# Row 0 of an attention and feed-forward kernel in two interleaved halves, with loads in queue order and a chain of released loads

One core of a Trainium2 chip. The metric is the device time of the whole kernel in microseconds (us), lower is better.

## What is computed

Attention over 8 rows of a batch (8 heads, 576 positions, head dimension 64), then a feed-forward product over all 4608 tokens. Cut to what matters:

```python
mask_plain = (rel >= 0) & (rel < 32)                        # heads 0 to 3: "sliding"
mask_dil = (rel >= 0) & (rel < 128) & (rel % 4 == 0)        # heads 4 to 7: "dilated"
attn = softmax(where(mask, q @ k.T / 8, -1e9));  x = attn @ v   # x: 4608 x 512
h = x @ w_in                                                # 512 -> 2048, "mm1"
r = maximum(h, 0); out = (r * r) @ w_out                    # 2048 -> 512, "mm2"
```

The feed-forward part goes by chunks of 512 tokens. Row 0 gives the tokens of chunk 0; attention of a later row runs on TensorE between the feed-forward matmuls of the chunk before it.

## The kernel before

The parts that the change touches (cuts marked with `...`). `idle()` issues filler matmuls whose result nobody uses, `pump(n)` issues the next n pieces of feed-forward work. In the profiles QKTp and QKTd are the transposed q and k of the sliding and the dilated heads, AT the attention weights, an AV product the weights times V, and xT the transposed result that mm1 reads. Half clock is also called cold.

```python
    load_sliding_qk(0, (nc.sync, nc.scalar))
    ...
    load_dilated_qk(0)
    load_sliding_v(0)
    load_dilated_v(0, nc.scalar)
    ...
    cast_sliding_qk(0, (nc.scalar, nc.scalar, nc.vector, nc.gpsimd))
    idle_matmuls(pj, 14, TOKC)
    ...
    transposes_and_scores(0, idle_and_load)     # w_in is issued in here
    scores_dilated(0, idle)
    cast_dilated_v(nc.scalar, DIL)
    xs = [av_sliding(0, 0)]
    ...
    x_dilated(0, 0, ys, False)
    load_sliding_qk(1)
    load_dilated_qk(1)
    g0 = hidden(0)
    pending.append(mm1_part_gen(0, g0, 0, 288))   # mm1 of the first 288 tokens
    zs = []
    for a in range(2):
        pump(1)
        zs.append(av_dilated(0, 1, a))            # ... beside the end of row 0
    ...
    load_w_out()
    pump(1000)
    pending.append(mm1_part_gen(0, g0, 288, TOKC))
    pump(2)
    reload_v(1)                                   # V of row 1
    ...
    cast_sliding_qk(1, (nc.scalar, nc.vector, nc.scalar, nc.vector))
    transposes_and_scores(1, lambda: pump(1))
    ...
    dk = keep_qk(2)                               # q and k of row 2
```

The softmax here doesn't subtract the row's maximum and nothing guards it: scores larger than these inputs give would overflow.

## Time and profile before

| | before |
|---|---|
| time, median of the 3 runs known then | 307.44 us (307.07 to 307.70) |
| the profiled run itself | 308.89 us, span 307.1 us |
| TensorE busy | 96% of the span |
| first mm1 matmul (chunk 0) | 24.84 us |
| first mm1 matmul of chunk 1 | 64.77 us |
| from there to the end of the span | 242.3 us |

From chunk 1 on TensorE sets the pace and the program is nearly the same in both kernels, so a change before chunk 1 can be read from one moment. I call it "the moment".

### The profile page before, as it was taken

The numbers are of one execution on the slowest core, as the hardware profiler recorded it, in microseconds if no ns is written. First come the engines' busy times: TensorE is split into PE (matmuls) and PEld (weight loads), VectorE is DVE, ScalarE is ACT, GpSimd is POOL, SyncE is SP. The second block draws the span as 40 slices with busy tenths as digits, with TensorE's granted clock in tenths as the row PEclk, the third lists the DMA queues.
The fourth block names the chain that finished last, engine by engine and source line by source line (L and its number), as shares of the span: only waits on it lengthen the run. The fifth ranks groups of instructions, "written<-read, shape, count | busy, mean of one in ns | idle before, by whom it ended". The sixth has DMA issues, their size and how long they took to land.

```text
span 307.1 us, 7069 instructions
## 1 busy us (share of the span) xinstructions
PE 295.0 (96%) x2920; PEld 199.0 (65%) x2920; DVE 213.7 (70%) x428; ACT 184.6 (60%) x317; POOL 41.9 (14%) x86
## 2 busy tenths in 40 slices
PE   6789999999899999999999999999999999999995
PEld 2777774444597459745974597459745974684484
DVE  5487682479976697769776977697769775834744
ACT  2586893668933894389438953895389526505610
POOL 4312302006002300230023002300100010000000
PEclk9599999999999999999999999999999999999998
DMA  7999899899979989999859993979520012003004
GB/s 183 249 210 226 142 179 211 186 224 224 276 147 240 266 143 221 226 225 155 178 168 226 152 231 113 228 173 181 142 96 2 0 40 99 2 0 140 0 0 139
DMA packets 83312, 47.91 MB, mean 156 GB/s; under 512 B 67792, under 2 KB 79568, under 8 KB 82896
## 3 DMA queue, kind: packets, MB, share of 16 engines
q1 hardware_dynamic: 75060, 26.12, 41.3%
q0 software_dynamic: 6848, 19.80, 28.3%
q10 hardware_dynamic: 1372, 1.54, 1.8%
q8 instruction: 23, 0.38, 0.5%
q14 instruction: 9, 0.07, 0.1%
HBM read 39.85 MB, written 16.52 MB: 184 GB/s over the span
## 4 chain that ended last, share of the span: by engine, by line
PE 86%; DMA 6%; ACT 3%; SPq 2%; DVE 1%; issue 1%; DVEq 0%; ACTq 0%
PE ph L324 37%; PE pob L374 9%; PE poa L374 9%; PE poe L374 5%; PE poc L374 5%; PE pod L374 5%; DMA sv<-in_v_dram 3%; PE paw L621 3%; PE ph L302 3%; DMA sq<-in_k_dram 2%; SPq L106 2%; PE pav L607 2%; PE py L654 2%; PE ps L556 1%; PE px L636 1%; PE po L345 1%
## 5 line engine op out<-in xcount | busy, mean ns | idle before, releaser
L324 PE MATMUL ph<-xT,wi 128*128 128x512 f16 x512 | 115.8, 379 | 0.0
L290 ACT ACTIVATE rt<-ph 128x512 f16<-128x512 f32 x128 | 75.5, 602 | 32.9 <-PE ph L324 32.6
L324 PEld LDWEIGHTS <-wi 128*128 128x128 f16 x512 | 48.2, 98 | 55.1
L294 DVE TENSOR_TENSOR g<-rt 128x1024 f16<-128x1024 f16 x56 | 38.7, 691 | 35.2 <-ACT rt L290 34.9
L374 PEld LDWEIGHTS <-sm 128*128 128x128 f16 x512 | 47.0, 98 | 4.9
L374 PEld LDWEIGHTS <-g 128*128 128x128 f16 x384 | 35.8, 98 | 6.5 <-DVE g L292 1.1
L374 PE MATMUL pob<-T,sm 128*128 128x256 f16 x256 | 32.5, 272 | 0.0
L374 PE MATMUL poa<-wo,g 128*128 128x256 f16 x256 | 32.1, 273 | 0.0
L660 ACT COPY xT<-py 128x576 f16<-128x576 f16 x16 | 10.2, 638 | 25.8 <-PE py L654 25.7
L394 POOL DMA_DIRECT2D out_dram<-otl x6 | 4.5, 756 | 152.2 <-DVE otl L429 152.2
L590 DVE TENSOR_TENSOR x_d<-paw,rcp_d 72x512 f16<-72x512 f32 x32 | 22.0, 686 | 1.1
L528 ACT ACTIVATE AT<-pz 128x576 f16<-128x576 f32 x32 | 19.0, 653 | 2.3 <-PE pz L575 1.8
L528 ACT ACTIVATE AT<-ps 128x576 f16<-128x576 f32 x32 | 19.2, 659 | 0.7 <-PE ps L538 0.3
L642 ACT COPY xT<-px 128x576 f16<-128x576 f16 x16 | 10.2, 640 | 14.7 <-PE px L636 14.7
L529 DVE TENSOR_TENSOR AT<-AT,maskp 128x576 f16<-128x576 f16 x32 | 14.9, 474 | 4.5 <-ACT AT L528 3.6
L302 PE MATMUL ph<-xT,wi 128*128 128x288 f16 (+1 forms) x128 | 16.6, 272 | 0.9 <-ACT xT L660 0.5
L590 DVE TENSOR_TENSOR x_p<-pav,rcp_p 96x512 f16<-96x512 f32 x24 | 16.5, 687 | 0.8
L529 DVE TENSOR_TENSOR AT<-AT,maskd 128x576 f16<-128x576 f16 x32 | 14.1, 456 | 3.4 <-ACT AT L528 2.3
L374 PE MATMUL pod<-T,g 128*128 128x256 f16 x128 | 16.2, 272 | 0.0
L374 PE MATMUL poc<-T,sm 128*128 128x256 f16 x128 | 16.2, 272 | 0.0
L374 PE MATMUL poe<-wo,sm 128*128 128x256 f16 x128 | 16.1, 273 | 0.0
L145 ACT CAST vd<-sd 128x1024 f16<-128x1024 f32 x16 | 16.1, 1070 | 0.0
(99 smaller groups left out, 369.7 us busy)
## 6 DMA issues: line engine op xcount, KB each, us to landing
sv<-in_v_dram SPq DMA_DIRECT2D x40, 128.0 KB, 4.6
sd<-in_v_dram SPq DMA_DIRECT2D x7, 512.0 KB, 5.9
dk<-in_k_dram POOLq DMA_DIRECT2D x12, 288.0 KB, 6.6
dk<-in_q_dram POOLq DMA_DIRECT2D x12, 288.0 KB, 8.2
out_dram<-otl POOLq DMA_DIRECT2D x6, 512.0 KB, 3.6
out_dram<-otu POOLq DMA_DIRECT2D x6, 512.0 KB, 3.7
wi<-in_moe_w_in_dram POOLq DMA_DIRECT2D x2, 1024.0 KB, 12.1
wo<-in_moe_w_out_dram POOLq DMA_DIRECT2D x4, 512.0 KB, 10.1
```

The source lines that it names most:

```text
L145: nc.scalar.copy(o, i)
L290: nc.scalar.activation(rt[:, o, :], ph[:], ACTF.Relu)
L294: nc.vector.tensor_mul(g[:, ffc - 1 : ffc + 1, :], rt, rt)
L302: nc.tensor.matmul(ph[:, 0 : t1 - t0], wi[:, dmk, ffc * P : ffc * P + P], xs[:, dmk, :], start=(dmk == 0), stop=(dmk == NDM - 1),)
L324: nc.tensor.matmul(ph, wi[:, dmk, ffc * P : ffc * P + P], xs[:, dmk, :], start=(dmk == 0), stop=(dmk == NDM - 1),)
L374: nc.tensor.matmul(acc, lhs[:, k, t * P : (t + 1) * P], rhs[:, k, :], start=(first and k == 0), stop=(k == NK - 1), skip_group_check=True,)
L528: nc.scalar.activation(AT[:, u, 0:UW], ps[:, :, 0 : UW // 2], ACTF.Exp, scale=scale)
L529: nc.vector.tensor_mul(AT[:, u, 0:UW], AT[:, u, 0:UW], mask)
L590: nc.vector.tensor_tensor(out=x[0:w], in0=pv[:, :, :, 0:D], in1=rcp[0:w].unsqueeze(3).to_broadcast([w, 2, HH, D]), op=ALU.mult,)
L621: nc.tensor.matmul(pav[:, e, h * (D + 2) : h * (D + 2) + D + 1], AT[:, 4 + h, off : off + P], vd[:, t, 2 * a + e, h, 0 : D + 1], start=Tru ...
L642: nc.scalar.copy(xT[:, 0:2, t0 : t0 + 288], px[:, 0:UW].rearrange("x (c t) -> x c t", c=2),)
L660: nc.scalar.copy(xT[:, 2:4, t0 : t0 + 288].rearrange("x c (i r) -> x c i r", r=DIL), py[:, 0:UW].rearrange("x (c r i) -> x c i r", c=2, r= ...
```

## The change

Its intent: start row 0 as soon as half of its q and k is there, let the second half load meanwhile, and let GpSimd issue each later load when it sees that an earlier one has landed. Core of the diff:

```diff
-    load_sliding_qk(0, (nc.sync, nc.scalar))
+    load_sliding_qk_half(0, 0, nc.sync)
+    load_sliding_qk_half(1, 0, nc.scalar)
...
-    load_dilated_qk(0)
+    load_dilated_qk_half(0)
+    load_dilated_v(0, nc.sync, (0,))
+    load_sliding_v(0, 0, 3)
+    load_sliding_qk_half(1, 1, nc.sync)
+    load_sliding_qk_half(0, 1, nc.sync)
+    load_sliding_v(0, 3, 6)
+    load_dilated_v(0, nc.sync, (1,))
     make_identity(nc, ident)
-    load_sliding_v(0)
-    load_dilated_v(0, nc.scalar)
+    load_dilated_qk_half(1)
...
+    def landed(x):
+        nc.gpsimd.tensor_copy(hold[0 : x.shape[0]], x)
+    (first half: casts, transposes, scores, AV products, with fillers)
+    x_sliding(0, 0, xs, False)
+    idle(6)
+    cast_sliding_qk_half(1, 1, nc.scalar)
+    cast_sliding_qk_half(0, 1, nc.scalar)
+    (second half the same way, with fillers)
+    load_w_out(0, 1)
+    landed(wi[:, NDM - 1, 1023:1024])
+    nc.gpsimd.memset(sq[:, :, :, 0:1], 0.0)
+    load_sliding_qk(1)
+    load_dilated_qk(1)
+    load_w_out(1, 4)
+    landed(wo[:, 3, DM - 1 :])
+    ... memsets of sv and sd
+    load_v(1)
+    landed(wo[:, NFF - 1, DM - 1 :])
+    landed(sd[:, 1, HH - 1, DIL * D - 1 :])
+    dk = keep_qk(2)
     g0 = hidden(0)
-    pending.append(mm1_part_gen(0, g0, 0, 288))
-    ... its pieces between the AV products of row 0
+    pending.append(mm1_gen(0, g0))                # unsplit, after row 0
+    pump(22)
     cast_sliding_qk(1, (nc.scalar, nc.vector, nc.scalar, nc.vector))
...  scores and dilated transposes of row 1 now lie beside mm2
```

Besides, w_in is loaded in four pieces instead of two, V of row 0 is cast on GpSimd alone, and in row 2 two pieces of feed-forward work are issued earlier.

## The prediction

> **What bounds the kernel now.** I read the page first: over the whole span TensorE is busy in 96%, and in the 40 slices only the first two are not full. The second slice (7.7 to 15.4 us) is also the only one with a halved TensorE clock.
>
> ```profile
> PE   6789999999899999999999999999999999999995
> ...
> PEclk9599999999999999999999999999999999999998
> DMA  7999899899979989999859993979520012003004
> ```
>
> From slice 9 on the rows of attention are hidden beside the feed-forward product and TensorE sets the pace: the seven-eighths products and the mm1 of a chunk repeat every 30.9 us in the chain. The change touches that part only by moving two fills in row 2. So what counts is one moment: when the first mm1 matmul of chunk 1 starts. All before it (row 0, chunk 0, row 1) is rewritten, all after it is kept. The timeline, and next to it the first matmuls of chunk 0:
>
> ```profile
> 24.84 0.41 PE L302 MATMUL ph<-xT,wi 128*128 128x288 f16 x2
> ...
> 28.96 7.47 PE L302 MATMUL ph<-xT,wi 128*128 128x288 f16 x64
> ...
> 64.77 7.52 PE L324 MATMUL ph<-xT,wi 128*128 128x512 f16 x34
> ```
>
> The moment is 64.77 us. The chain of waits says what led to the first useful matmuls, and later through row 0:
>
> ```profile
> 0.75 7.51 DMA sq<-in_k_dram
> 8.26 0.03 issue
> 8.28 0.96 DVE early L147
> 9.24 0.05 issue
> 9.29 0.66 PE pt L499 x6
> ...
> 16.66 1.10 ACT AT L528 x2
> ...
> 18.48 2.19 ACT AT L528 x4
> ```
>
> The reader sees 8.3 us of waiting for q and k of row 0, then a cast, then the transposes. The table of windows shows what that wait does to TensorE, and that the DMA engines are full from 3 us on:
>
> ```profile
> 5.00:10.00 5.00, 2.06 (x15) 1.16 (x14) 1.32 (x7) 1.56 (x2) 0.82 (x1) 0.86 1.16 239
> 10.00:15.00 5.00, 5.00 (x61) 4.66 (x60) 1.91 (x4) 2.36 (x4) 2.14 (x4) 0.50 1.19 258
> 15.00:20.00 5.00, 4.45 (x99) 3.85 (x97) 4.13 (x10) 4.13 (x11) 1.27 (x3) 0.96 1.16 211
> ```
>
> Between 10 and 15 us TensorE is busy throughout at clock 0.50: it is its own bound there, for some 3 us more than the same instructions would need at full clock. A third stretch: V of row 1 lands at 54.4 us (18 us after issue), but queued mm2 matmuls fill most of that wait.
>
> **What the Trainium skill says.** "TensorE: Matmul & The Clock Gate", section "What's actually happening", says that the array falls to half clock after an idle window of about 3.4 us and gets it back after a busy one. The trace agrees in kind: the filler matmuls end at 6.35 us, the next starts at 9.29, and the clock is 0.50 from 9 to 15 us; it was lost at about 8.6, so after 2.3 us of idling. "DMA: Bandwidth & Descriptors", section "Issuing engines are not separate DMA queues", says that all issuers share 16 engines. It agrees: with three queues issuing, the total stays at 213 to 295 GB/s from 3 to 20 us; order, not the number of queues, decides what lands first. "GPSIMD Engine Reference", section "4.1 Engine selection", has one-input work on GpSimd at roughly line rate; here GpSimd casts 96x768 in 0.82 us against 0.95 on VectorE, so the V casts moved there cost nothing extra.
>
> **The change part by part.** (1) First loads halved. q and k of half a row are 0.59 MB instead of 1.18. By the rates of the windows (12, 152, 295, 275 GB/s), 1.5 MB had moved at 8.3 us, of which 1.18 were q and k; half of it, 0.74 MB, had moved at 5.0. So q and k land near 5.2 us. VectorE is then held by its setup: it ended at 5.4, and the memset of QKTd grows from 64 to 640 words a partition, some 0.55 us by the rate of the 256-word one (0.27 us): 6.0. The 13 fillers end at 6.1. The first half starts 3.2 us earlier, and the idle gap of 2.9 us is gone, so TensorE stays at full clock: another 3 us of the cold stretch.
>
> (2) Against that, the row now runs as two chains one after the other. I followed the changed order with durations of the trace: cast 0.83 (ScalarE) and 0.95 (VectorE), QKTp copy 0.64 and 0.76, a pair of QKTd copies 0.70 and 0.81, exp 0.60, mask 0.50, normalise 0.90 (0.55 for one tile), xT copy 0.64, 0.4 to 0.5 from a matmul's start to its reader. First half: casts done 6.95, copies 8.1 and 8.4, QKTd 9.75, four exps until 11.45, last mask 12.0. V of it (0.64 MB behind q) should land near 10 and be cast on GpSimd by 11.4 and 12.6. AV products 11.6 to 13.3, xT copy of the sliding part done 15.05. Second half: ScalarE's two casts come after that copy in its order, 15.05 to 16.65; QKTp copies to 17.7 and 18.35; exp 18.35 to 18.95; xT copy 19.6; exp 20.2; mask 20.75; QKTd copies 21.55; two exps to 23.2; mask 23.75; four normalises to 26.9; transposes and xT copy: first mm1 at T0 = 28.0. The other bound is TensorE's own queue: 84 fillers of 128 columns at 0.09 us (five take 0.45) are 7.6 us, about 196 small matmuls some 8 us (six transposes 0.33, eight AV products 0.3, sixteen score products 0.31): from 6.1, T0 = 22. Fillers look chosen near the real waits, so I lean a little below my chain: T0 = 26.7.
>
> (3) Chunk 0 is no longer split. Before, 64 matmuls of 288 columns (52 in 6.17 us, 0.119 each) and 64 of 224 (0.10) are 14.0 us; 64 of 512 (34 in 7.36 us, 0.2165) are 13.9. The split cost nothing in TensorE's time, but it allowed 20 matmuls, 2.4 us, to run before row 0 was finished. This overlap is given up.
>
> (4) The rest up to chunk 1. From the end of the first split part, 36.43, to 64.77 are 28.3 us: 44 short mm1 matmuls (4.4 us), row 1 and mm2. The changed kernel needs the 23.9 without those, plus 13.9 for mm1: chunk 1 starts at T0 + 37.8. Equality with 64.77 is T0 = 27.0. Here the change should also win a little: between 40 and 45 us ScalarE was busy for 5.00 of 5 us with relu, exp and copies together; scores and dilated transposes now lie beside mm2, where it has slack, and the one V wait (VectorE's 5.9 us, under a us of it on TensorE) goes if V of row 1 is released by the first w_out piece near 32 us. I put this at 0.6 us. Sum: 26.7 + 37.8 - 0.6 = 63.9, that is 0.9 us earlier: 307.4 - 0.9 = 306.5.
>
> (5) Released loads: none should be late. w_in is issued near 13 us, and its second half is needed at T0 + 7; the q and k of row 1 are released by the second w_in piece near 22 and need some 11 us at half the rate, against a use at T0 + 9.5; row 2's transposes follow as before.
>
> **The rivals.** First, the author's intent holds in full: T0 near 22 to 24, the two halves really overlap, chunk 1 starts 3 to 5 us earlier, 302.5 to 304.5. For it: the fillers, and 6 us of start and clock that are really there to be had. Against it: each half passes all of exp, mask, AV and normalise, and the ScalarE order puts the second half's casts behind the first half's xT copy. Second, the serial chain holds or gets worse: TensorE waits about 2 us near 20 us between the fillers and the second QKTd copies; as 2.3 us of idling lost the clock before, it can be lost again, which adds 1 to 2 us: T0 28 to 30, 308.5 to 310.5. Third, loads become the bound: sliding V comes in small packets and w_in competes with the last V of row 0. In the kernel before, GpSimd's V casts waited for V until 17.05 us; if V of the second half lands after 23, or the chained releases leave DMA engines idle, each us is paid. The full DMA row speaks for little slack, the 0.72 between 30 and 35 us for some.
>
> **Range and chances.** A low of 302.5 is T0 at 23 with the 0.6 and some more of the later stalls removed; a high of 310.5 is T0 at 29.5 with a further us of waits. Faster by over 2% means under 301.3, chunk 1 at 58.6, T0 under 21.5: below even TensorE's own queue, 0.09. Slower by over 2% means over 313.6, 6 us lost, only by a lost clock and late loads together: 0.05. Within 2%: 0.86.
>
> **What would show it.** Right: first transposes near 6.1 us at full clock; no slice at 0.5; exp of the first half done near 11.5; second casts behind the first xT copy near 15; first mm1 at 26 to 28; first mm1 of chunk 1 at 63 to 65; the rest as long as before (242.3 us). Wrong: the first mm1 under 24 (halves overlap more than I think), a clock of 0.5 near 20 us, a DMA wait ahead of mm1, or a part after chunk 1 that changes by over a us.

## The result

| | before | after |
|---|---|---|
| time, median (range) of 4 runs each | 307.57 us (307.07 to 308.44) | 310.10 us (309.85 to 310.78) |
| profiled run, its span | 308.89 us, 307.1 us | 310.78 us, 309.0 us |
| first mm1 matmul | 24.84 us | 29.27 us |
| the moment | 64.77 us | 66.52 us |
| from the moment to the end | 242.3 us | 242.5 us |

The ratio is 1.0083, with a 95% interval of 1.0054 to 1.0111. A ratio here is the mean time of one kernel's fast runs over that of the other's of the same rounds, so not quite the ratio of the medians quoted. The changed kernel is 0.8% slower, the same by the measure of 2%.

The page of the changed kernel, in 40 slices:

```profile
PE   7759999999989999999999999999999999999995
...
PEclk9796999999999999999999999999999999999999
DMA  8999998799989969899949992999430003003003
```

Its start is earlier, but now there are two cold places (the 7 and the 6 in the row of the clock) instead of one. The DMA row looks as full as before; the windows below show a gap in it. TensorE's timeline (start, duration, engine, line, operation; in brackets the wait before it and what ended it):

```profile
6.42 0.68 PE L566 MATMUL ph<-ident,early 96*128 96x96 f16 x12 [0.54 <-ACT early L166]
7.66 0.42 PE L584 MATMUL pg<-ident,early 72*128 72x72 f16 x8 [0.33 <-DMA early<-in_k_dram]
...
10.32 0.42 PE L584 MATMUL pg<-ident,early 72*128 72x72 f16 x8 [2.01 <-DMA early<-in_q_dram]
...
17.67 0.30 PE L566 MATMUL ph<-ident,early 96*128 96x96 f16 x3 [1.12 <-ACT early L166]
...
22.48 0.97 PE L664 MATMUL pz<-QKTd 64*128 64x72 f16 x16 [1.44 <-DVE QKTd L168]
...
29.27 10.53 PE L359 MATMUL ph<-xT,wi 128*128 128x512 f16 x48
...
45.61 1.47 PE L380 MATMUL po<-wo,g 128*128 128x512 f16 x6
```

The first transposes start at 6.42 us against 9.29 before: the 2.9 us are won. But the first mm1 comes at 29.27 us against 24.84. Between them stand a new wait of 2.0 us for the dilated q, and the waits at 17.67 and 22.48 us for the second half, which began late. ScalarE's timeline shows why:

```profile
12.06 1.19 ACT L599 ACTIVATE AT<-pz 128x576 f16<-128x576 f32 x2 [0.39 <-PE pz L664]
16.25 0.64 ACT L735 COPY xT<-px 128x576 f16<-128x576 f16 x1 [3.00 <-PE px L729]
16.78 1.56 ACT L166 CAST early<-sq 96x768 f16<-96x768 f32 x2
...
23.24 1.19 ACT L599 ACTIVATE AT<-pz 128x576 f16<-128x576 f32 x2 [1.68 <-PE pz L664]
27.96 0.64 ACT L735 COPY xT<-px 128x576 f16<-128x576 f16 x1 [3.53 <-PE px L729]
```

The two casts of the second half stand behind the copy of the first half's result, for which ScalarE waits 3.0 us with nothing to do. The table of windows, cut at the moments where the clock changed (the columns are the window, its length, busy times of PE, PEld, DVE, ACT and POOL, the granted clock, the DMA share, GB/s; the share is packet time over the time of 16 engines and can pass 1):

```profile
8.08:11.49 3.41, 1.40 (x29) 1.03 (x29) 1.16 (x3) 1.72 (x4) 0.00 (x0) 1.00 1.21 214
11.49:14.90 3.41, 3.35 (x49) 3.14 (x47) 3.25 (x6) 1.38 (x3) 2.03 (x2) 0.50 1.24 207
14.90:18.32 3.42, 1.95 (x38) 1.55 (x36) 2.35 (x7) 2.07 (x3) 2.81 (x5) 1.00 0.73 162
18.32:21.73 3.41, 2.42 (x51) 1.91 (x51) 1.42 (x4) 2.85 (x6) 2.90 (x4) 1.00 1.24 205
21.73:25.14 3.41, 2.54 (x39) 2.32 (x40) 2.15 (x7) 1.19 (x2) 0.80 (x3) 0.50 1.24 207
25.14:28.55 3.41, 3.41 (x44) 3.41 (x42) 2.73 (x7) 0.59 (x1) 3.21 (x6) 0.50 1.22 222
```

The clock is at half for 10.2 us up to the moment, against 6.8 us in the kernel before. The DMA share falls to 0.73 from 14.90 to 18.32 us. GpSimd holds w_in until it sees the second half's q (15.46 us) and then takes 3.0 us to issue four pieces from 15.70 us; the kernel before issued w_in at 12.90 us, and its share stayed at 1.12 or more from 13 to 20 us.

### The profile page after: what moved, and what is told of

Same layout as the page of the kernel before. It is cut to its first block, busy times and chain, and to the rows that moved or that the text cites. A ratio compares the mean times of both kernels' runs of the same rounds, so it can differ in the third digit from the quotient of the medians.

```text
span 309.0 us, 6928 instructions
## 1 busy us (share of the span) xinstructions
PE 295.5 (96%) x2857; PEld 193.6 (63%) x2857; DVE 214.4 (69%) x418; ACT 182.5 (59%) x299; POOL 48.8 (16%) x97
## 2 busy tenths in 40 slices
DMA packets 85615, 47.89 MB, mean 155 GB/s; under 512 B 68112, under 2 KB 82896, under 8 KB 85200
## 4 chain that ended last, share of the span: by engine, by line
PE 90%; ACT 4%; DMA 2%; issue 1%; DVE 1%; POOL 1%; ACTq 0%; POOLq 0%
PE ph L359 41%; PE pob L409 9%; PE poa L409 9%; PE poe L409 5%; PE poc L409 5%; PE pod L409 4%; PE po L380 4%; PE paw L714 3%; PE pav L697 2%; DMA early<-in_q_dram 2%; PE pj L509 2%; PE pz L646 2%; PE px L729 1%; PE ps L627 1%; PE py L747 1%; ACT AT L599 1%
## 5 line engine op out<-in xcount | busy, mean ns | idle before, releaser
L359 PE MATMUL ph<-xT,wi 128*128 128x512 f16 x576 | 130.5, 379 | 0.0
L325 ACT ACTIVATE rt<-ph 128x512 f16<-128x512 f32 x144 | 85.0, 601 | 35.8 <-PE ph L359 35.5
L359 PEld LDWEIGHTS <-wi 128*128 128x128 f16 x576 | 54.2, 98 | 61.7
L329 DVE TENSOR_TENSOR g<-rt 128x1024 f16<-128x1024 f16 x63 | 43.5, 691 | 44.4 <-ACT rt L325 44.1
L678 DVE TENSOR_TENSOR x_p<-pav,rcp_p 96x512 f16<-96x512 f32 (+1 forms) x25 | 16.6, 665 | 0.9
L380 PE MATMUL po<-wo,g 128*128 128x512 f16 x64 | 17.0, 379 | 0.0
L677 DVE RECIPROCAL rcp_d<-paw 72x8 f32<-72x8 f32 x32 | 6.3, 198 | 13.1 <-PE paw L714 13.1
```

What stands on the lines that cost most here:

```text
L325: nc.scalar.activation(rt[:, o, :], ph[:], ACTF.Relu)
L329: nc.vector.tensor_mul(g[:, ffc - 1 : ffc + 1, :], rt, rt)
L359: nc.tensor.matmul(ph, wi[:, dmk, ffc * P : ffc * P + P], xs[:, dmk, :], start=(dmk == 0), stop=(dmk == NDM - 1),)
L380: nc.tensor.matmul(po, g[:, ffc, t * P : (t + 1) * P], wo[:, ffc, :], start=(ffc == 0), stop=(ffc == NFF - 1),)
L677: nc.vector.reciprocal(rcp[0:w, 0:n], pv[:, :, :, D])
L678: nc.vector.tensor_tensor(out=x[0:w, 0:n], in0=pv[:, :, :, 0:D], in1=rcp[0:w, 0:n].unsqueeze(3).to_broadcast([w, n, HH, D]), op=ALU.mult,)
```

## The experiments

Theories ahead of them. (A) Row 0 became a chain: ScalarE's order and the wait for the dilated q make the second half late. (B) The overlap of mm1 with the end of row 0 is missed. (C) The lost clock costs the time. (D) The new order of loads and of row 1 costs time later on. (E) The DMA engines deliver what they can; an earlier start of row 0 only waits elsewhere. A rival to (E) was not tested: the held issue of w_in, and not full engines, makes the loads late.

All twelve runs, with the two kernels, and the moment of each profiled run:

| kernel | median us | ratio to before [95%] | first mm1 | the moment | span | span less moment |
|---|---|---|---|---|---|---|
| before | 307.57 | | 24.84 | 64.77 | 307.1 | 242.3 |
| before_again | one look | | 24.87 | 64.18 | 306.5 | 242.3 |
| after | 310.10 | 1.0083 [1.0054, 1.0111] | 29.27 | 66.52 | 309.0 | 242.5 |
| c_after_warm | 310.70 | 1.0123 [1.0099, 1.0147] | 29.46 | 66.72 | 309.2 | 242.5 |
| d_v_later | 311.61 | 1.0149 [1.0126, 1.0172] | 31.03 | 68.28 | 310.7 | 242.4 |
| e_casts_early | 309.46 | 1.0052 [1.0029, 1.0076] | 27.56 | 64.82 | 307.3 | 242.5 |
| b_mm1_fill | 308.50 | 1.0047 [1.0033, 1.0060] | 21.58 | 64.46 | 306.9 | 242.4 |
| a_rest_only | 308.33 | 1.0051 [1.0030, 1.0072] | 26.82 | 65.06 | 307.6 | 242.5 |
| h_overlap_newrest | 308.65 | 1.0032 [1.0009, 1.0056] | 23.72 | 65.65 | 308.2 | 242.6 |
| h_warm | 308.49 | 1.0039 [1.0008, 1.0070] | 22.46 | 65.36 | 308.0 | 242.6 |
| g_before_warm | 307.63 | 1.0015 [0.9999, 1.0031] | 22.70 | 63.80 | 306.1 | 242.3 |
| k_qk_first | 307.98 | 1.0000 [0.9972, 1.0027] | 22.92 | 63.03 | 307.3 | 244.3 |
| l_no_v_hold | 308.14 | 1.0016 [0.9991, 1.0042] | 22.68 | 62.74 | 305.3 | 242.6 |
| m_halves_best | 307.75 | 1.0000 [0.9982, 1.0019] | 21.29 | 64.55 | 307.0 | 242.4 |

The last column is the check of the method: in every trace but one the rest takes 242.3 to 242.6 us, so the moment explains the span. A traced run is one sample (kernel l's runs go from 307.10 to 309.32 us, the traced one is the fastest; m's go from 307.28 to 308.77, the traced one is the slowest; the traced runs of after, d, h and k are the slowest of theirs too, e's is nearly the fastest). So the moments are compared for their causes and the ratios for the size. A ratio compares with the kernel before in the same rounds; the medians come from different rounds, and in part from different chips (0, 1 and 10).

**c_after_warm: fillers in the two gaps (theory C).** An inconclusive run.

```diff
+    idle(28)                       # ahead of the transposes of the dilated q, half 0
-    idle(6)                        # ahead of the dilated scores of half 1
+    idle(26)
```

> The changed kernel with 28 fillers ahead of the second dilated transposes (TensorE waited 2.0 us there for q) and 26 instead of 6 ahead of the second half's dilated scores (1.4 us of waiting). If the lost clock (0.50 from 11.3 to 14.9 and from 21.7 to 28.5 us) is what made the changed kernel slower, first mm1 at 27.5 to 28.3 instead of 29.27 and 1 to 1.7 us shorter, near the kernel before. If the two serial chains on ScalarE and VectorE make the length of row 0, the gain is under 0.8 us.

The clock was kept through the first gap, and the second half's first transposes came at 16.91 us instead of 17.67. But then the clock was lost at 17.4 us, before the second batch of fillers began; these ran at half speed and held the dilated scores until 23.62 us, although the copies that the scores need had ended at 22.42. The first mm1 came at 29.46 us:

```profile
14.00:17.41 3.41, 1.70 (x31) 1.34 (x29) 2.48 (x7) 1.93 (x3) 2.48 (x5) 1.00 1.20 232
17.41:20.82 3.41, 3.18 (x47) 2.69 (x48) 1.28 (x3) 2.76 (x6) 3.23 (x4) 0.50 1.20 200
20.82:24.24 3.42, 3.42 (x45) 3.12 (x43) 1.19 (x3) 0.53 (x2) 0.23 (x2) 0.50 1.24 208
```

So it does not say what a row 0 at full clock throughout would give. With the first half at full clock the second half started 0.8 us earlier in this one trace. Fillers ahead of the two waits were not enough here: the clock went in the stretch between them.

**d_v_later: V of row 0 issued from 5.4 us instead of 2.5, so that the dilated q comes first (theory A or E).**

```diff
-    (memsets of sv, sd and the six loads on nc.sync, early)
     nc.vector.memset(AT[:, :, UW:640], 0.0)
+    (the same memsets and loads here)
```

> The changed kernel with V of row 0 and the second half's q and k issued from SyncE near 5 us instead of 2.5, so that the dilated q of the first half, for which TensorE waited 2.0 us until 10.3, meets less traffic. If that wait was only a matter of order, q lands near 8, the first half is 1.5 to 2 us earlier, and the whole 1 to 1.5 us shorter. If the DMA engines are simply full, V and the second half land later by as much and the first mm1 stays at 29 to 30 us: no change in the time or up to 1 us longer.

The wait for the dilated q was gone, and V came too late instead. The waits of TensorE (total, times, longest):

```profile
PE pav L697 <- POOL vp L168: 2.9, 1, 2.9
PE pz L664 <- DVE QKTd L168: 1.5, 2, 1.0
```

First mm1 at 31.03 us, the ratio up to 1.0149, clear of the changed kernel's interval. Putting one load first made another late. That no order would do is not shown: with the later issue the engines moved only 117 to 140 GB/s from 5 to 7 us, against 217 to 221 in the changed kernel, so this edit lost transfer time as well as changing the order.

**e_casts_early: the two casts of the second half ahead of the first half's copy on ScalarE (theory A).**

```diff
+    cast_sliding_qk_half(1, 1, nc.scalar)
+    cast_sliding_qk_half(0, 1, nc.scalar)
     x_sliding(0, 0, xs, False)
     idle(6)
-    cast_sliding_qk_half(1, 1, nc.scalar)
-    cast_sliding_qk_half(0, 1, nc.scalar)
```

> The changed kernel with ScalarE's two casts of the second half ahead of the first xT copy, where it idled for 3.0 us. The last q of the second half landed at 15.45 us, the casts ran from 16.78. If the ScalarE order set the second half's start (as the prediction had it), the casts run at 15.5 to 17.1, first mm1 1 to 1.3 us earlier, time 0.8 to 1.3 us shorter. If the second half is bound further on, by VectorE's masks and normalises and the lost clock, the gain is under 0.4 us.

ScalarE's and then TensorE's timeline:

```profile
15.50 0.83 ACT L166 CAST early<-sq 96x768 f16<-96x768 f32 x1 [0.85 <-DMA sq<-in_q_dram]
```

```profile
21.42 0.96 PE L664 MATMUL pz<-QKTd 64*128 64x72 f16 x16 [2.33 <-DVE QKTd L168]
...
27.56 10.53 PE L359 MATMUL ph<-xT,wi 128*128 128x512 f16 x48
```

The casts end at 16.33 us instead of 18.34, and the first mm1 and the moment come 1.7 us earlier than in the changed kernel. In the traces theory A is a cause, but only part of the gain in the casts arrives: VectorE's copies of the second half (QKTd) are the next wait, 2.3 us. VectorE has them behind two mask products that wait for ScalarE's exps, so its order does there what ScalarE's did. In time the ratios are 1.0083 and 1.0052 (about 1 us), with intervals that overlap.

**b_mm1_fill: the changed kernel with mm1 of the first 288 tokens beside the second half, where the fillers were (theory B).**

```diff
-    idle(6)
+    g0 = hidden(0)
+    pending.append(mm1_part_gen(0, g0, 0, 288))
+    pump(2)
     xs += av_sliding(0, 3, 5)
     ... each following idle(...) becomes pump(2) or pump(1)
-    pending.append(mm1_gen(0, g0))
-    pump(22)
+    pump(1000)
+    pending.append(mm1_part_gen(0, g0, 288, TOKC))
+    pump(10)
```

> The changed kernel with mm1 of the first 288 tokens put where the second half has fillers, and mm1 of the other 224 beside row 1, as the kernel before has it. If the lost overlap is the cause, mm1 of chunk 0 ends 3 to 4.5 us earlier than in the changed kernel. Then, if nothing else binds, the time falls by 3 to 4 us, to about 306. If the loads of row 1 bind (V landed at 54.0), the AV products of row 1 start at 55.5 to 56.5 instead of 57.84 and the gain stops at 1.5 to 2.3 us, with a new wait for V.

```profile
21.58 2.10 PE L337 MATMUL ph<-xT,wi 128*128 128x288 f16 x8 [1.09 <-DMA wi<-in_moe_w_in_dram]
...
43.53 1.47 PE L380 MATMUL po<-wo,g 128*128 128x512 f16 x6
```

The first mm1 is 7.7 us earlier, but these run at half clock and among small work; what counts is the first mm2, at 43.53 instead of 45.61 us, and the moment, 2.06 us earlier. In time it is about 1.1 us by the ratios (1.0083 to 1.0047), whose intervals hardly meet; the expected 3 to 4 us did not come. In the moment theory B's part is the largest of those taken alone, but the ratios do not separate it from run e's (1.0052) or run a's (1.0051).

**a_rest_only and h_overlap_newrest: row 0 of the kernel before, the new order of row 1 and of the loads (theory D).** Kernel a has fillers where mm1 was; kernel h keeps the split mm1 beside row 0.

```diff
 (row 0 as before; a: idle() for each pump, h: the pumps kept)
+    load_w_out(0, 1)
+    landed(wi[:, NDM - 1, 1023:1024])
+    ... the chain of released loads and row 1 as in the changed kernel
```

> Row 0 of the kernel before (one piece, fillers instead of mm1 between its AV products), with the changed kernel's order from chunk 0 on: unsplit mm1, scores beside mm2, loads released one by one. If the split into halves is what costs, first mm1 at 28 to 28.5 and the time 1 us under the changed kernel. If the rest of the change costs, the time is that of the changed kernel although row 0 is the old one; the changed kernel needs 37.25 us from its first mm1 to chunk 1, and I expect 37 to 37.5 here as well unless the loads come later.

> Row 0 in one piece and mm1 of its first 288 tokens beside its AV products, as in the kernel before; from there on the changed kernel's loads and order. With the earlier runs this separates three parts: changed kernel to b_mm1_fill is the overlap (measured 1.1 us), b_mm1_fill to this one is the halving of row 0, this one to the kernel before is the new order of loads and scores. If the halving costs, this is 1 to 1.5 us faster than b_mm1_fill, 307 or below. If the new order of the rest is what costs, it stays at b_mm1_fill's 308.5.

Kernel a has its first mm1 at 26.82 us, 2.45 us before the changed kernel's, and needs 38.2 us from there to the moment instead of the expected 37 to 37.5: the k of row 1 is waited for until 37.8 us. Its ratio is 1.0051 against the changed kernel's 1.0083, in intervals that overlap. With row 0 whole and its overlap kept (h), the new rest is still 0.3% slower than the kernel before, and its moment is 65.65 us although its first mm1 is 1.1 us earlier than there. So theory D has a share once row 0 is earlier; the changed kernel took 37.25 us from first mm1 to the moment, as predicted. Kernel b, halved, and kernel h, whole, otherwise much alike, differ by 0.15% (1.0047 and 1.0032, in intervals that overlap): where mm1 is overlapped, the halving neither gains nor loses anything that these runs resolve.

**h_warm, and k_qk_first: where the new rest loses.** h_warm is h with 26 fillers at the start instead of 14, which keeps the clock until q and k land. k has, besides, the q and k of row 1 ahead of the first piece of w_out.

```diff
-    load_w_out(0, 1)
     landed(wi[:, NDM - 1, 1023:1024])
     ... q and k of row 1
-    load_w_out(1, 4)
+    load_w_out(0, 4)
```

> The same with 26 fillers, so that the clock is kept until the first transposes. The released loads leave no gap in the DMA engines at 30 to 36 us, so V of row 1 should land near 51 us instead of 54.4, and the earlier row 0 can be used: first mm1 of chunk 1 at 62 to 63, 305.5 to 306.5. If the loads bind here too, the same as without the added fillers.

> h_warm with the first w_out piece issued after the q and k of row 1 instead of before. In h_warm TensorE stood nearly still from 35.2 to 38.5 us, because the casts of row 1 waited for its k until 36.6 and the clock fell with it. If the place of w_out in the queue is what made the changed kernel's release order cost 1.3 us, k lands near 34.5 to 35.5, that gap shrinks to 1 us or less, chunk 1 starts at 62 to 63.5 and the time is 304.5 to 306.5, at or under the kernel before. If the DMA engines were simply full whichever order, k lands at 36 to 37 again and the time stays at 308.

ScalarE's cast of row 1's q and k, in h_warm and then in k:

```profile
36.64 1.56 ACT L145 CAST early<-sq 96x768 f16<-96x768 f32 x2 [2.25 <-DMA sq<-in_k_dram]
```

```profile
35.70 1.56 ACT L145 CAST early<-sq 96x768 f16<-96x768 f32 x2 [0.86 <-DMA sq<-in_k_dram]
```

With q and k first the wait shrinks by 1.4 us, the moment comes 2.3 us earlier (63.03 instead of 65.36), and the ratio goes from 1.0039 to 1.0000, in intervals that overlap. Part of the 2.3 us is the clock: in h_warm it was also lost after this wait, from 39.35 to 42.76 us, in k it was kept. So in these traces a piece of w_out ahead of row 1's q and k is a loss of theory D; the time does not resolve it. Yet k is no faster than the kernel before, and its trace, taken of the slowest of six runs, is the one row of the table with 244.3 us of rest. ScalarE's timeline and the chain of waits of k show where:

```profile
86.11 1.04 ACT L145 CAST vd<-sd 128x1024 f16<-128x1024 f32 x1 [3.33 <-DMA sd<-in_v_dram]
88.49 1.04 ACT L145 CAST vd<-sd 128x1024 f16<-128x1024 f32 x1 [1.34 <-DMA sd<-in_v_dram]
```

```profile
74.74 13.74 DMA sd<-in_v_dram
```

V of row 2 lands late, and chunk 2 begins at 96.91 us, no earlier than in the kernel before (96.75). GpSimd had seen V of row 1 land at 52.15 us and only then issued the q and k of row 2, although the last piece of w_out was there at 45.8; run l below takes that hold away. The hold alone is not the reason: h_warm issued them at 52.71 us too, and its V of row 2 was not waited for. There the last V load was issued at 71.60 us and took 6.9 us, here at 74.74 us and 13.7 us; why is open.

**g_before_warm: the kernel before with 26 fillers instead of 14.**

```diff
-    idle_matmuls(pj, 14, TOKC)
+    idle_matmuls(pj, 26, TOKC)
```

> The kernel before with 26 instead of 14 fillers ahead of the first transposes, so that TensorE does not lose its clock between 8.6 and 15.3 us. If the chain of row 0 sets the end, row 0 is done some 2 to 3 us earlier (first mm1 of chunk 0 near 22.5 instead of 24.84, if w_in has landed) and the whole is 1.5 to 2.5 us shorter. If the loads set the end (V of row 1 lands at 54.4 us in the kernel before and at 54.0 in the changed one, although the schedules differ), the first mm1 of chunk 1 moves by less than 0.5 us and the time stays within 0.5 us.

The cleanest evidence for theory E: here no load is held by a new chain. The clock is kept, the first mm1 comes at 22.70 us instead of 24.84, and then:

```profile
53.59 1.47 ACT L145 CAST vp<-sv 128x1536 f16<-128x1536 f32 x1 [4.47 <-DMA sv<-in_v_dram]
```

V of row 1 lands when it lands; before it, mm1 had waited 1.05 us for w_in. Of the 2.1 us, 0.4 to 1.0 are left at the moment (63.80 against 64.18 and 64.77), and nothing in the time: 1.0015, with 1 just inside the interval.

**before_again: the kernel before, as a base for traces.**

> The kernel before once more, for a second trace: the profiled run of the first trace had a span of 307.1 us at a mean granted clock of 0.986, while the runs timed since had 305.3 at 0.994. The chain and the DMA theories both expect the same instruction order; I expect the cold stretch (8.6 to 15.3 us in the first trace) to be about one 3.4 us window shorter and the first mm1 of chunk 1 near 63.0 instead of 64.77.

The expected shorter cold stretch did not come. It is the same picture as the first trace (V of row 1 waited for 3.7 us on ScalarE, moment 64.18): 0.6 us of the moment is scatter between these two runs.

**l_no_v_hold: k without GpSimd's wait for V of row 1 ahead of row 2's q and k.**

```diff
     landed(wo[:, NFF - 1, DM - 1 :])
-    landed(sd[:, 1, HH - 1, DIL * D - 1 :])
     dk = keep_qk(2)
```

> The run with row 1's q and k ahead of the first w_out piece (row 0 whole and overlapped), with one line less: GpSimd no longer waits for V of row 1 before it issues the q and k of row 2, only for the last w_out piece. In that run the issue came at 52.6 us and chunk 2 began at 96.9 us although chunk 1 had begun at 63.0; the DMA engines were busy for only 0.64 of 48 to 54 us. My theory (the gain at chunk 1 is given back because the loads of row 2 are chained to V of row 1): issue near 46 us, V of row 2 landed by about 85 us instead of 88.5, chunk 2 at 95 to 96 us, span and time 0.7 to 1.5 us shorter than that run, so ratio to the kernel before 0.995 to 0.998. Rival (the DMA engines are the limit, whatever the order): V of row 1 lands about as much later as q and k of row 2 move earlier, the vp cast waits for V by 2 us or more, chunk 1 starts at 64 to 65 us, and the ratio stays 0.999 to 1.003.

The window from 48 to 54 us in k and then in l:

```profile
48.00:54.00 6.00, 5.88 (x65) 2.85 (x62) 2.65 (x6) 4.45 (x9) 1.55 (x4) 1.00 0.64 116
```

```profile
48.00:54.00 6.00, 5.68 (x58) 2.64 (x57) 2.65 (x6) 4.45 (x9) 0.62 (x2) 1.00 1.16 252
```

The gap in the DMA engines (share 0.64, 116 GB/s) is filled (1.16, 252 GB/s). In the traced run the moment (62.74 us) is kept through row 2 and the span is 305.3 us. But that run was the fastest of six, and the ratio of 1.0016 lies in the range of the rival. The expected gain was not shown: what filled the gap is certain, that it pays is not.

**m_halves_best: the changed kernel with all edits that had helped.**

```diff
 b_mm1_fill, and
+    the two casts ahead of x_sliding(0, 0), as in e
+    q and k of row 1 ahead of w_out, as in k
-    landed(sd[:, 1, HH - 1, DIL * D - 1 :])
```

> The changed kernel (two halves) with every single edit that helped it, together: mm1 of the first 288 tokens beside the second half in place of the fillers, the two casts of the second half ahead of the first xT copy on ScalarE, row 1's q and k ahead of the first w_out piece, and no hold on V of row 1. Alone, the first two gave 310.1 to 308.5 and 309.5, and the third moved chunk 1 by 2.3 us in another variant. My theory (the losses of the change are these steps and they add): first mm1 at 20 to 21 us, first mm2 at 41 to 42, chunk 1 at 61.5 to 63 us, time 305.5 to 307, ratio 0.993 to 0.999. Rival (the start is set by what the DMA engines have delivered, so an earlier row 0 only waits for w_in, for q and k of row 1 or for V): waits of 2 us or more for these in front of mm1 or row 1, chunk 1 at 63.5 to 64.5 us, ratio 1.000 to 1.004.

The ratio is 1.0000 (0.9982 to 1.0019), clear of the changed kernel's interval: the loss of the changed kernel is gone, so its cause lies in the four things that this run repairs together, and nothing is gained over the kernel before. It is also clear of b's interval (1.0033 to 1.0060): the casts and the loads gain about 1.4 us more than b by the ratios, on another chip. In the traced run, the slowest of six, the moment, 64.55 us, is not earlier than in b (64.46). TensorE's and then ScalarE's timeline:

```profile
21.29 2.10 PE L337 MATMUL ph<-xT,wi 128*128 128x288 f16 x8 [2.64 <-DMA wi<-in_moe_w_in_dram]
```

```profile
22.47 0.41 ACT L347 ACTIVATE rt<-ph 128x288 f16<-128x288 f32 x1 [2.97 <-PE ph L337]
23.43 0.41 ACT L347 ACTIVATE rt<-ph 128x288 f16<-128x288 f32 x1 [0.55 <-PE ph L337]
23.79 1.19 ACT L599 ACTIVATE AT<-pz 128x576 f16<-128x576 f32 x2
```

The second half is ready sooner, but its first mm1 pieces wait 2.6 us for w_in; ScalarE, in order, waits behind them for 3.0 us before it comes to the last exps of row 0, and the clock is lost (half from 20.7 to 27.5 us). The ratio and the trace fell where the rival, a start that waits for the DMA engines, had put them; my 0.993 to 0.999 was wrong. Whether full engines make w_in late is not shown: here too GpSimd issued it from 15.69 us, behind the hold for q, and the DMA share fell to 0.68, with 62 GB/s, from 17 to 18 us. No run issues w_in earlier. How the gain over b divides between the casts and the loads stays open as well.

## Why the prediction was right or wrong

The range (302.5 to 310.5) held the time, and "within 2%" was right. But the time lies only 0.4 us inside the high end, which the second rival had set. The lean to a small gain was wrong, in direction too: 306.5 predicted, 310.1 measured.

- **The method, the moment:** right. The rest took 242.5 us in the changed kernel against 242.3.
- **(1) The earlier start:** right in size (6.42 us for a predicted 6.1), wrong about what follows from it. "TensorE stays at full clock" failed: the dilated q landed 2.0 us late for its transposes, and the clock was lost at 11.5 us instead of 8.6.
- **(2) The chain by hand, 28.0:** right in its steps but for one that it lacked. The last exp of the first half ended at 13.25 us (I had 11.45), the copy at 16.89 (15.05), the second casts followed it as I had written, the last QKTd copies ended at 22.78 (21.55), the first mm1 began at 29.27. The chain came 1.3 us later than by hand, and the wait for the dilated q, which was not in it, is the step where it fell behind (by 1.8 us, 0.6 of which came back later).
- **The failed step** is the next sentence: "Fillers look chosen near the real waits, so I lean a little below my chain: T0 = 26.7." Nothing in a trace stood behind it. The equality that I had worked out was 27.0, so my own chain of 28.0 said "slower"; run e, which removes the order of ScalarE that I had seen, still starts mm1 only at 27.56.
- **(3) The overlap given up:** right, and in size too. I gave it 2.4 us of matmuls, and it is in the sum of (4), where all of mm1 follows T0, its first matmul. Run b gets 2.06 us back at the moment and about 1.1 in the time. One reading was loose: the line of 64 matmuls at 28.96 us holds 44 of 288 columns and 20 of 224 (44 of the 64 short ones come later), so "52 in 6.17 us" mixes both. The sum hardly moves.
- **(4) T0 + 37.8 less 0.6:** right. The moment was T0 + 37.25. The wait for V of row 1 did go. That the first w_out piece ahead of row 1's q and k costs something once row 0 is earlier, as k shows, I did not see; it was hidden in the changed kernel, whose row 0 is late.
- **(5) "None should be late":** wrong for the first loads (dilated q), right for w_in and V of row 1 in the changed kernel.
- **The base:** the trace of before that I subtracted from was a run of 308.89 us, and I set its moment equal to the median of 307.4. With that the miss of 3.6 us adds up: 2.6 from the moment (66.52 for 63.9), 1.45 from this base, 0.2 from the rest, less 0.7, because the traced run of the changed kernel is also above its median.
- **The rivals:** the second, a serial chain with a clock lost again near 20 us (T0 28 to 30, 308.5 to 310.5), is what happened, clock and all. The size of the clock's part was not isolated (c had 0.8 us for the first half). The third, loads as the bound, is what the traces of g, k and m show in front; in k and m it is not shown whether full engines or held issues make the loads late. The prediction had named the second of these too: "the chained releases leave DMA engines idle".

So the earlier start of 2.9 us went, in this order: into the wait for the dilated q, into a second half queued behind the first on ScalarE, and into an mm1 that begins only when row 0 is complete. Run m shows that repairing the last two, with two edits of the loads, removes the loss; the share of each rests on one trace apiece.

## What to carry to other kernels

When the DMA engines are full from the first microseconds on, splitting the first loads can move the wait to another load, as here to the dilated q; look for the next load that will be late before counting the gain. When a stage is split into two halves, look at the order of every engine: a first step of the second half that stands behind a wait of the first half keeps the halves from overlapping (ScalarE's casts, then VectorE's copies). Fillers in such gaps may be worth replacing by useful work (about 1.1 us in run b). Compare a change with the median run's base and not with a single trace, and do not move a chain worked out by hand without a reason that a trace shows.

## What the Trainium skill lacked or had wrong

- "TensorE: Matmul & The Clock Gate", section "What's actually happening": its free-running window of about 3.4 us agrees with these traces better than my reading in the prediction ("after 2.3 us of idling"). In the changed kernel the clock changed at 11.49, 14.90, 21.73 and 28.55 us, that is after 3.41, 6.83 and 6.82 us; the half-clock stretches last 6.83 us in the kernel before and 17.07 us (five windows) in d. The page does not say how idle an "idle window" is. Here the clock was lost after windows with 1.17 (before), 1.40 (after), 1.70 (c), 1.28 (d), 1.63 and 1.27 us (m) of TensorE work in 3.41 us, and kept after 1.95. It came back after windows with 3.35 us or more, in e after 3.15 and in h after 3.18, but not after 3.18 (c) or 3.17 (d). So busy time alone does not give a threshold; nor does it for the loss: 2.42 us of work in the changed kernel, and the clock was lost after it.
- "DMA: Bandwidth & Descriptors", section "Issuing engines are not separate DMA queues": agrees (in run d, with SyncE's loads issued later, GpSimd's pieces of the dilated q took 4.5 us to land instead of 7.4), but gives no rate for a mix such as this one. Between 6 and 30 us the engines of the changed kernel had a share of 1.15 and more in most windows, at 200 to 260 GB/s, with a gap from 15 to 18 us (share 0.51 to 0.92); 68112 of the changed kernel's 85615 packets were under 512 bytes.
- No page that I read for this case tells what it costs that a held issue on GpSimd holds all issues after it. In k, w_out had landed at 45.8 us, but the q and k of row 2 were issued at 52.6, behind a hold for V, and the DMA share fell to 0.64 from 48 to 54 us; without the hold it was 1.16.
